# Scatter token numbers, expert 1's second matrix in four pieces, and routing sums ahead of the turns

## The chip, the cores and the metric

The kernel runs on one core of one Trainium2 chip. The core has five instruction streams that run side by side and wait for one another through semaphores: TensorE (PE in the profile, with its weight loads as PEld), VectorE (DVE), ScalarE (ACT), GpSimd (POOL) and SyncE (SP, which here only issues DMA transfers). Each stream works in its own order: an instruction that waits holds back everything behind it on that engine. TensorE writes into PSUM banks, of which the program has eight.

The metric is the device time of one execution, in microseconds, and the median over executions.

## The reference

A long convolution along the sequence is followed by a layer of eight experts of which every token uses one.

```python
X = np.fft.rfft(x, axis=1)                      # x: 8 x 3072 x 256
y = np.fft.irfft(X * (filt_r + 1j * filt_i)[None], n=3072, axis=1)
x = y.reshape(24576, 256)
logits = x @ w_gate                             # 8 experts
expert_idx = np.argmax(logits, axis=1)
gate_w = softmax(logits)[chosen expert]
...
for i in range(N):                              # first 768 tokens of each expert
    e = expert_idx[i]
    if counts[e] < capacity:                    # capacity 768
        disp[e, counts[e]] = x[i]; pos[i] = counts[e]; counts[e] += 1; keep[i] = True
h = np.maximum(np.einsum('ecd,edf->ecf', disp, w1), 0.0)   # w1: 8 x 256 x 1024
y = np.einsum('ecf,efd->ecd', h, w2)                       # w2: 8 x 1024 x 256
out[i] = gate_w[i] * y[expert_idx[i], pos[i]]   # 0 for tokens that were not kept
```

## The kernel before

Only the first tokens of each expert count, so the kernel convolves three batches of eight (the third for half of its rows), routes their tokens, and computes the experts; a branch at the end does the whole again if an expert was not full by then, which does not happen with these inputs.

**The order of the work is the order of the code.** The whole kernel stands in a manual schedule: each engine gets its instructions in the order in which the Python code emits them, and the framework adds the waits. The functions named below emit; `run` calls a list of emitters, `interleave` mixes lists.

**A batch's convolution.** `rows_in` (lines 889 to 895) emits the first transform (matmuls L273, copies to `ZA`). `cv.t(k)`, the turns, transpose `ZA` into `Q` (matmuls L296, copies L301 on ScalarE); there are six. `cv.middle` (from line 360) then goes through six groups g of frequencies, each in two halves h. `b(g, h)` emits the matmuls L309 on `Q`, four VectorE products L325 for the two halves of a group, and a subtraction and an addition on GpSimd (L329, L330) that give `t`. `g(u)` emits twelve matmuls L342 on `t` and copies `yh`, `yl`; it needs up to two groups' `t`, both halves. `bi(u)` emits nine matmuls L356 and copies into `V`. `middle` takes a list `fill` of other work and puts one item of it behind each half group. After the middle come the transposes `ti`, and the second inverse transform `ai` or, for the last batch, `ai_last` (matmuls L414, L440, copies to `rt`, DMA writes of `rt` to `ybuf`).

**Routing.** `route` returns lists: `counts` (VectorE: argmax, one-hot, running sums, ending in `ends`), `sums` (five small matmuls, L509 to L512, on `ends`), `slots` (VectorE, from L517 on), `masks` (one-hot tables for the index table, L560 to L562) and `table` (matmuls L570, then a finish into `tacc`, a table that has for every slot of every expert its row in `ybuf`). For batches 0 and 1, `cv.t(0)` is emitted between `counts` and `sums`.

**Token numbers.** Rows of `ybuf` are not in token order. `row_of_slot` makes gather indices from `tacc` with one VectorE instruction. `scatter_rows(ix, n)` (lines 696 to 725) makes the token numbers, to which results are scattered, with eighteen VectorE instructions in a chain. For the first twelve columns of the table (experts 0 and 1, `idxs0`) it is called in `early_index`, an item of `fill` in the last batch's middle; for all 48 (`idxs`) it is called after the convolution, ahead of expert 1's first up steps.

**Experts.** Slots come in chunks of 384. `gather` brings a chunk's rows with three indirect DMAs on GpSimd (L590). `turn` transposes them on TensorE (L604) and splits them into a high and a low part, `xh` by ScalarE (L611) and `xl` by VectorE (L615). An up step is six matmuls L630 (high by high, low by high, high by low), a ReLU split into `h` (L611 ScalarE, L613 VectorE); a chunk has eight. A down step is 24 matmuls L681 and a scaled copy `ob` (L684); `scatter` is an indirect DMA on GpSimd (L687). Expert 0's first chunk and expert 1's first chunk are computed early, from the first two batches' tokens, among the last batch's transforms.

**Weights.** `load_part` loads a matrix (1 MB) into a raw tile and splits it in parts by `cut`: `wah` (or `wbh`) by a ScalarE copy, the low part by a GpSimd subtraction (L744, for expert 1's first matrix), or by a ScalarE negation (L746) and a later accumulating DMA (L750). The pool `raw0` has one buffer, so expert 1's second matrix goes where its first matrix lay. Before, it comes as one DMA that GpSimd issues (L737) after the four subtractions. ScalarE's order there is: two copies `rt`, two cuts of the second matrix, two copies `rt`, a cut, an `ob`, a cut, and then `xh` of the turn of expert 1's first chunk.

Of the kernel before, what the change touches and what calls it, by code (L numbers as in the profile page):

```python
# [9 lines left out]
F32 = mybir.dt.float32  # L10
# [11 lines left out]
N1, N2, NP = 96, 32, 24  # L22
# [71 lines left out]
def fftconv_moe_kernel(ctx, tc, x, x0, fr, fi, fny, wg, w1, w2, ca, cai, cb, co, out, cap):  # L94
    nc = tc.nc
    NB, SEQ, D = x.shape[0], N1 * N2, 256
    E, FF = w1.shape[0], w1.shape[2]
    NT = (cap + 127) // 128
    NSLOT = E * NT
# [63 lines left out]
    def interleave(*lists):  # L163

        marks = sorted(((i + 1) / (len(l) + 1), j, i) for j, l in enumerate(lists) for i in range(len(l)))
        for _, j, i in marks:
            lists[j][i]()

    def run(fs):
        for f in fs:  # L170
            f()
# [521 lines left out]
    def down(k, ix=None):  # L693
        run(down_steps(k, ix))
# [31 lines left out]

    def load_part(e, part, raw, pool, parts=2, dma=None, add=True, adds=None):

# [6 lines left out]
        def load():  # L735
            box.append(raw.tile(shape, F32, name="raw", tag="raw"))
            (dma or nc.sync).dma_start(out=box[0], in_=src)  # L737

        def cut(k):
# [101 lines left out]
    with tc.manual_schedule():  # L841
# [55 lines left out]
        for b in range(NB0 - 1):  # L897
# [10 lines left out]
            interleave(rows_in(b + 1, range(4, 8), False), counts)  # L908
            cv.t(0)
            sums()  # L910
            interleave([lambda k=k: cv.t(k) for k in range(1, NP // 4)], slots)
            if b + 2 == NB0:
# [17 lines left out]
        def early_index():  # L930
            early_count()
            row_of_slot(idx0, EE * NT)
            scatter_rows(idxs0, EE * NT)

# [20 lines left out]
        adds, scatters = [], []  # L955
        load_a, cut_a = load_part(1, "a", raw0, w1p, 4, add=False)
        load_b, cut_b = load_part(1, "b", raw0, w1p, 4, nc.gpsimd, adds=adds)
        load_a()
        L = new_L(True)
# [13 lines left out]
        run([early[4], cut_a[0], early[5], cut_a[1], early[6], cut_a[2], early[7], cut_a[3]])  # L973
        load_b()
        for q in range(2, 4):
# [7 lines left out]
        sums()  # L983
        run(scatters[:1])
        run(cut_b[:2])
# [3 lines left out]
        later[1]()  # L989
        run(scatters[1:2])  # L990
        run(cut_b[3:])
        run(masks)
        X[1, 0] = turn(early_x[1], NE, ep1)
        later[2]()
# [15 lines left out]
        R[1, 1] = load_rows(1, 1)  # L1010
        scatter_rows(idxs, NSLOT)

# [13 lines left out]
        load_a()  # L1026
        down((1, 0), idxs0)
        up((1, 1), list(cut_a), 1)
        down((0, 1))
# [117 lines left out]
```

## Time and profile before

| | |
|---|---|
| median of 3 runs | 489.73 us |
| the runs | 489.97, 489.73, 486.75 us |
| the profiled execution, its own time | 493.15 us |
| its span in the trace | 491.3 us |
| mean granted clock of TensorE | 0.991 of full speed |
| TensorE busy | 473.9 us, 96% of the span |
| VectorE, ScalarE, GpSimd busy | 49%, 54%, 40% of the span |

TensorE is busy almost throughout; matmuls are pipelined, so busy says that matmuls are under way, not that they go at full speed. The granted clock says at which of its two levels, 1.2 or 2.4 GHz, TensorE ran: 1.00 is 2.4 GHz, 0.50 is 1.2 GHz. A row of the timeline has its start, its duration, engine, line, operation, tiles, shape, and in brackets how long the engine was idle before it and what ended that.

### The profile page before, as it was taken

How to read it: one execution, taken by the hardware profiler on the slowest of the kernel's cores; microseconds unless marked ns; L12 is line 12 of the kernel's file. 1: busy time of each engine (PE TensorE's matmuls, PEld its weight loads, DVE VectorE, ACT ScalarE, POOL GpSimd, SP SyncE). 2: the span in 40 equal slices, each digit the busy share in tenths (PEclk: the TensorE clock that was granted, in tenths of full speed). 3: DMA queues.
4: the chain of work that ended last, by engine and by line, in shares of the span. 5: the costliest groups of instructions: out<-in, count | busy, mean ns of one | idle time of the engine just before them, and what ended most of it. 6: DMA issues, size and time to landing. Idle time of an engine off the chain costs nothing.

```text
span 491.3 us, 10853 instructions
## 1 busy us (share of the span) xinstructions
PE 473.9 (96%) x4317; PEld 462.2 (94%) x4317; DVE 240.2 (49%) x562; ACT 264.7 (54%) x618; POOL 198.8 (40%) x241
## 2 busy tenths in 40 slices
PE   8999999999999899989999999999999999999994
PEld 8999998999989799979899999999999899999994
DVE  3587755776557788847422343233332323423510
ACT  3555767356576587554362684374383482573421
POOL 3064210552104674618432654355354454454022
PEclk9999999999999899999999999999999999999999
DMA  8996180990817738547348699979979989985001
GB/s 291 391 312 257 33 234 4 256 345 2 234 39 211 171 61 179 141 144 152 82 141 233 145 235 268 357 196 273 355 213 263 362 211 271 376 159 123 1 24 48
DMA packets 59980, 95.72 MB, mean 195 GB/s; under 512 B 4016, under 2 KB 36496, under 8 KB 59792
## 3 DMA queue, kind: packets, MB, share of 16 engines
q1 hardware_dynamic: 43264, 63.27, 39.6%
q0 software_dynamic: 15344, 29.56, 28.2%
q10 hardware_dynamic: 1312, 2.10, 1.3%
q8 instruction: 36, 0.59, 0.5%
q14 instruction: 24, 0.20, 0.1%
HBM read 54.81 MB, written 40.11 MB: 193 GB/s over the span
## 4 chain that ended last, share of the span: by engine, by line
PE 48%; issue 21%; POOL 11%; DMA 11%; ACT 4%; DVE 2%; POOLq 1%; SPq 0%; ACTq 0%
PE ps L630 9%; PE ps L273 9%; DMA y<-ob,idxs 7%; PE ps L681 7%; PE ps L342 6%; PE ps L309 6%; PE ps L414 5%; PE ps L356 5%; POOL y L687 4%; POOL rows L590 3%; DMA raw<-w 2%; POOL wal L750 2%; PE ps L296 1%; POOL wbl L750 1%; DMA V<-x 1%
## 5 line engine op out<-in xcount | busy, mean ns | idle before, releaser
L681 PE MATMUL ps<-wbh,h 128*128 128x256 f32 x768 | 139.5, 281 | 0.2
L613 DVE SCALAR_TENSOR_TENSOR h<-ps,h 128x384 fp32r<-128x384 f32 x128 | 66.8, 553 | 120.1 <-ACT h L611 99.6
L681 PEld LDWEIGHTS ps<-wbh,h 128*128 128x128 f32 x768 | 119.1, 189 | 1.1 <-issue 0.7
L681 PE MATMUL ps<-wbl,h 128*128 128x256 f32 x384 | 107.6, 280 | 0.4 <-issue 0.4
L687 POOL DMA_INDIRECT y<-ob,idxs x48 | 48.1, 1003 | 115.0 <-ACT ob L684 108.6
L630 PE MATMUL ps<-xh,wah 128*128 128x384 f32 x256 | 87.2, 341 | 3.7 <-ACT xh L611 2.0
L630 PE MATMUL ps<-xl,wah 128*128 128x384 f32 x256 | 87.0, 340 | 0.6 <-DVE xl L615 0.2
L630 PE MATMUL ps<-xh,wal 128*128 128x384 f32 x256 | 86.6, 338 | 0.0
L611 ACT ACTIVATE h<-ps 128x384 fp32r<-128x384 f32 x128 | 58.8, 497 | 46.2 <-PE ps L630 38.4
L681 PEld LDWEIGHTS ps<-wbl,h 128*128 128x128 f32 x384 | 72.7, 189 | 0.9 <-issue 0.9
L684 ACT ACTIVATE ob<-ps,gt 128x256 f32<-128x256 f32 x48 | 22.1, 477 | 77.3 <-DMA y<-ob,idxs 36.7
L630 PEld LDWEIGHTS ps<-xh,wah 128*128 128x128 f32 x256 | 48.6, 190 | 4.9 <-ACT ob L684 2.6
L329 POOL TENSOR_TENSOR t<-t,t 128x256 f32<-128x256 f32 x33 | 24.9, 753 | 67.8 <-DVE t L325 63.4
L630 PEld LDWEIGHTS ps<-xl,wah 128*128 128x128 f32 x256 | 48.6, 190 | 1.4 <-DVE xl L615 0.9
L630 PEld LDWEIGHTS ps<-xh,wal 128*128 128x128 f32 x256 | 48.7, 190 | 0.0
L590 POOL DMA_INDIRECT rows<-ybuf,idxg x42 | 42.4, 1009 | 15.1 <-issue 12.2
L342 PE MATMUL ps<-IG,t 128*128 128x136 f32 x288 | 39.0, 285 | 2.5 <-POOL t L330 2.4
L345 ACT CAST yh<-ps 128x408 fp32r<-128x408 f32 x48 | 23.9, 502 | 29.7 <-PE ps L342 28.4
L342 PEld LDWEIGHTS ps<-IG,t 128*128 128x128 f32 x288 | 36.3, 194 | 3.2 <-POOL t L330 3.1
L309 PE MATMUL ps<-Bc,Q 128*128 128x128 f32 x288 | 36.3, 278 | 0.0
L615 DVE TENSOR_TENSOR xl<-ps,xh 128x384 fp32r<-128x384 f32 x32 | 16.2, 547 | 38.8 <-ACT xh L611 30.5
L309 PEld LDWEIGHTS ps<-Bc,Q 128*128 128x128 f32 x288 | 33.8, 192 | 0.9 <-issue 0.7
(142 smaller groups left out, 746.0 us busy)
## 6 DMA issues: line engine op xcount, KB each, us to landing
y<-zt SPq DMA_DIRECT2D x12, 2048.0 KB, 20.1
raw<-w SPq DMA_DIRECT2D x13, 1024.0 KB, 7.1
wbl<-w POOLq DMA_DIRECT2D x16, 512.0 KB
wal<-w POOLq DMA_DIRECT2D x14, 512.0 KB
xt<-x SPq DMA_DIRECT2D x16, 384.0 KB, 4.5
ybuf<-rt SPq DMA_DIRECT2D x12, 256.0 KB, 4.6
ybuf<-rt SPq DMA_DIRECT2D x14, 204.0 KB, 3.5
Q<-x SPq DMA_DIRECT2D x4, 528.0 KB, 9.2
```

What stands on the lines that cost most here:

```text
L273: nc.tensor.matmul(ps[:, i * w:(i + 1) * w], xt[:, i, h * 128:(h + 1) * 128], A[:, i * QP:i * QP + w], start=True, stop=True)
L309: nc.tensor.matmul(ps[:, i * 128:(i + 1) * 128], self.Q[:, p, h * 128:(h + 1) * 128], self.Bc[:, 1 if p == NP - 1 else 0, :], start=True, ...
L329: eng.tensor_tensor(out=t1[:, :, 0, :], in0=t1[:, :, 0, :], in1=t2[:, :, 1, :], op=ALU.subtract)
L342: nc.tensor.matmul(ps[:, i * 136:(i + 1) * 136], self.ysb[(p // 4, h)][:, (p % 4) * 128:(p % 4 + 1) * 128], self.IG[:, h, :], start=True, ...
L356: nc.tensor.matmul(ps[:, :272], w[:, m, :], y[:, i, :], start=k == 0, stop=k == 2)
L414: nc.tensor.matmul(ps[s * rows:(s + 1) * rows, i * w:(i + 1) * w], AI[:, o, r0:r0 + rows], V[h][:, :w // 2, o, :], start=True, stop=True)
L590: nc.gpsimd.indirect_dma_start(out=rows[:, t, :], out_offset=None, in_=yrows[:lim, :], in_offset=bass.IndirectOffsetOnAxis(ap=idx[:, j + t ...
L611: nc.scalar.activation(out=hi, in_=ps, func=AF.Relu if relu else AF.Copy)
L613: nc.vector.scalar_tensor_tensor(out=lo, in0=ps, scalar=0.0, in1=hi.bitcast(F32), op0=ALU.max, op1=ALU.subtract)
L630: nc.tensor.matmul(ps[:, :n * 128], w[:, kk, m * 128:(m + 1) * 128], y[:, kk, o], start=k == 0, stop=k == 5)
L681: nc.tensor.matmul(ps[:, :D], y[:, m, o], w[:, m, :], start=m == 0 and j == 0, stop=m == NF - 1 and j == 2)
L687: ins = nc.gpsimd.indirect_dma_start(out=out, out_offset=bass.IndirectOffsetOnAxis(ap=(idxs if ix is None else ix)[:, j:j + 1], axis=0), i ...
```

## The change

Five edits, all in the order of emission but one. (1) `early_index` no longer calls `scatter_rows(idxs0, ...)`; it is called after `masks` of the last batch, and the first two scatters of expert 0 are emitted right behind it instead of where their `ob` is made. (2) `scatter_rows(idxs, NSLOT)` moves from ahead of expert 1's up steps to behind the down steps of its first chunk. (3) Expert 1's two matrices share one flat raw tile; the second comes in four pieces of 256 KB on SP's queue, each into the quarter that one cut of the first matrix has read, in place of one load on GpSimd's queue. (4) In batches 0 and 1 `sums()` is emitted ahead of all turns. (5) With that, the six turns, not five, are interleaved with `slots`.

```diff
-    def load_part(e, part, raw, pool, parts=2, dma=None, add=True, adds=None):
+    def load_part(e, part, raw, pool, parts=2, dma=None, add=True, adds=None, flat=None):
...
+        def load_piece(k, parts):
+            n = shape[1] // parts
+            nc.sync.dma_start(out=box[0][:, k * n:(k + 1) * n, :], in_=src[:, k * n:(k + 1) * n, :])
+
+        if flat is not None:
+            box.append(flat.rearrange("p (n f) -> p n f", f=shape[2]))
+            load = load_piece
...
-            cv.t(0)
             sums()
-            interleave([lambda k=k: cv.t(k) for k in range(1, NP // 4)], slots)
+            interleave([lambda k=k: cv.t(k) for k in range(NP // 4)], slots)
...
             row_of_slot(idx0, EE * NT)
-            scatter_rows(idxs0, EE * NT)
...
-        load_a, cut_a = load_part(1, "a", raw0, w1p, 4, add=False)
-        load_b, cut_b = load_part(1, "b", raw0, w1p, 4, nc.gpsimd, adds=adds)
-        load_a()
+        flat = raw0.tile([128, 8 * D], F32, name="raw", tag="raw")
+        load_a, cut_a = load_part(1, "a", raw0, w1p, 4, add=False, flat=flat)
+        load_b, cut_b = load_part(1, "b", raw0, w1p, 4, adds=adds, flat=flat)
+        load_a(0, 1)
...
-        load_b()
+        for k in range(4):
+            load_b(k, 4)
...
         sums()
-        run(scatters[:1])
         run(cut_b[:2])
...
         later[1]()
-        run(scatters[1:2])
         run(cut_b[3:])
         run(masks)
+        scatter_rows(idxs0, EE * NT)
+        run(scatters[:2])
         X[1, 0] = turn(early_x[1], NE, ep1)
...
         R[1, 1] = load_rows(1, 1)
-        scatter_rows(idxs, NSLOT)
...
         down((1, 0), idxs0)
+        scatter_rows(idxs, NSLOT)
```

The first place is VectorE in the last batch's middle, behind the table's finish. Before, the end of the eighteen instructions (te, tf and up are their work tiles) and then the products of group 2:

```order
L722 TENSOR_SCALAR up<-at 128x12
L706 SCALAR_TENSOR_TENSOR tf<-up,tf 128x12
L724 TENSOR_SCALAR te<-tacc 128x12
L725 TENSOR_TENSOR idxs_73<-te,tf 128x12
L325 TENSOR_TENSOR t_2356<-ps,FRT 128x512
```

and now:

```order
L451 TENSOR_SCALAR tb<-tb 128x1
L830 TENSOR_TENSOR tot<-tot,lack 128x2
L140 TENSOR_SCALAR idx_72<-tacc 128x12
L325 TENSOR_TENSOR t_2335<-ps,FRT 128x512
L325 TENSOR_TENSOR t_2336<-ps,FIT 128x512
```

The eighteen instructions are gone from there; the products stand right behind the gather index. They come back on VectorE between the one-hot tables of the last batch and the low part `xl` of expert 1's turn, whose end is now:

```order
L722 TENSOR_SCALAR up<-at 128x12
L706 SCALAR_TENSOR_TENSOR tf<-up,tf 128x12
L724 TENSOR_SCALAR te<-tacc 128x12
L725 TENSOR_TENSOR idxs_73<-te,tf 128x12
L615 TENSOR_TENSOR xl<-ps,xh 128x6x64 x2
L575 TENSOR_TENSOR tacc<-tacc,pr 128x48
```

where before L615 followed the one-hot tables directly. The second place is GpSimd behind the four subtractions for expert 1's first matrix. Before:

```order
L744 TENSOR_TENSOR wal<-raw,wah 128x512 x4
L737 DMA raw<-w 128x8x256
L445 COPY L<-rt_2860 128x48
L445 COPY L<-rt_2879 128x48
L445 COPY L<-rt_2898 128x32
L687 DMA y<-ob,idxs_73 24576x256 x2
L590 DMA rows<-ybuf,idxg 128x264 x3
```

On SP's queue, between the load of expert 1's first matrix and the last batch's writes, stands now:

```order
L741 DMA raw<-w 128x2x1024
L741 DMA raw<-w 128x2x256 x4
L446 DMA ybuf<-rt_2841 128x6x136
L446 DMA ybuf<-rt_2860 128x6x136
L446 DMA ybuf<-rt_2879 128x4x136
```

The load has left GpSimd's row and become four on SP's, ahead of five writes to `ybuf`; the two scatters keep their place in GpSimd's row, between the copies of the logits and the gathers, but wait there for `idxs0`.

## Rows read from the trace of the kernel before

**Rows 1.** The page, part 1: busy time of each engine.
```profile
PE 473.9 (96%) x4317; PEld 462.2 (94%) x4317; DVE 240.2 (49%) x562; ACT 264.7 (54%) x618; POOL 198.8 (40%) x241
```
**Rows 2.** Windows of 3 us: stretch, length, busy by engine, clock, DMA share, GB/s.
```profile
169.00:172.00 3.00, 3.00 (x16) 3.00 (x15) 0.64 (x2) 1.57 (x8) 2.68 (x4) 0.51 0.85 135
220.00:223.00 3.00, 3.00 (x11) 3.00 (x10) 2.20 (x13) 1.10 (x3) 2.06 (x2) 0.50 0.18 45
```
**Rows 3.** Timeline, TensorE, middles of batch 1 and of the last batch.
```profile
92.57 1.56 PE L342 MATMUL ps<-IG,t 128*128 128x136 f32 x12
...
105.54 1.95 PE L309 MATMUL ps<-Bc,Q 128*128 128x128 f32 x16
...
156.11 1.56 PE L342 MATMUL ps<-IG,t 128*128 128x136 f32 x12
...
167.99 0.50 PE L342 MATMUL ps<-IG,t 128*128 128x136 f32 x2 [2.22 <-POOL t L330]
...
173.58 1.95 PE L309 MATMUL ps<-Bc,Q 128*128 128x128 f32 x16
```
**Rows 4.** Timeline, VectorE, last batch's middle: first of eighteen, and what follows them.
```profile
159.54 0.17 DVE L708 TENSOR_SCALAR tf<-tacc 128x12 f32<-128x12 f32 x1
...
162.44 0.68 DVE L325 TENSOR_TENSOR t<-ps,FRT 128x512 f32<-128x512 f32 x1
```
**Rows 5.** Timeline, GpSimd, last batch's middle: group 2's first, group 3's last operation.
```profile
163.81 0.72 POOL L329 TENSOR_TENSOR t<-t,t 128x256 f32<-128x256 f32 x1 [3.13 <-DVE t L325]
...
173.54 0.74 POOL L330 TENSOR_TENSOR t<-t,t 128x256 f32<-128x256 f32 x1
```
**Rows 6.** Timeline, TensorE, start of expert 1's first chunk.
```profile
216.28 0.17 PE L827 MATMUL ps<-tot,ones 128*1 128x10 f16 x1
218.47 0.44 PE L630 MATMUL ps<-xh,wah 128*128 128x384 f32 x1 [2.02 <-ACT xh L611]
...
228.02 0.59 PE L604 MATMUL ps<-ident,rows 64*128 64x64 f32 x12
```
**Rows 7.** Chain that ended last: eight up steps, start and duration.
```profile
249.31 8.32 PE ps L630 x48
```
**Rows 8.** Timeline, ScalarE, ahead of expert 1's first chunk.
```profile
207.46 0.59 ACT L442 COPY rt<-ps 128x512 f32<-128x512 f32 x1 [0.47 <-PE pr L512]
212.06 0.62 ACT L742 CAST wbh<-raw 128x512 fp32r<-128x512 f32 x1 [4.01 <-DMA raw<-w]
...
217.55 0.87 ACT L611 ACTIVATE xh<-ps 128x384 fp32r<-128x384 f32 x2
```
**Rows 9.** Timeline, GpSimd: four subtractions, then the load.
```profile
196.46 5.08 POOL L744 TENSOR_TENSOR wal<-raw,wah 128x512 fp32r<-128x512 f32 x4 [1.54 <-ACT wah L742]
...
201.83 0.94 POOL L737 DMA_DIRECT2D raw<-w  x1 [0.30 <-POOL wal L744]
```
**Rows 10.** Timeline, VectorE, end of the one-hot tables and the low part.
```profile
212.10 0.35 DVE L562 TENSOR_TENSOR ohh<-ohh,nv 128x384 f16<-128x384 f16 x1
218.07 1.02 DVE L615 TENSOR_TENSOR xl<-ps,xh 128x384 fp32r<-128x384 f32 x2 [5.61 <-ACT xh L611]
```
**Rows 11.** Timeline, GpSimd: the last of twelve gathers in a row.
```profile
239.23 1.00 POOL L590 DMA_INDIRECT rows<-ybuf,idxg  x1 [0.31 <-issue]
```
**Rows 12.** DMA, 238 to 244 us in forty slices: busy tenths.
```profile
DMA  0096271000398450000991740000000000000000
```
**Rows 13.** Timeline, batch 0: first turn, the read of the sums, first table.
```profile
77.29 0.28 PE L296 MATMUL ps<-ident,ZA 64*128 64x64 f32 x2
...
78.83 0.17 DVE L517 COPY bs<-pr 128x16 f32<-128x16 f32 x1 [4.25 <-PE pr L512]
...
83.75 0.38 PEld L570 LDWEIGHTS <-ol 128*128 128x128 f16 x8 [0.20 <-DVE ohh L560]
```
**Rows 14.** Windows of 5 us, columns as in group 2.
```profile
245.00:250.00 5.00, 5.00 (x42) 5.00 (x41) 0.43 (x1) 1.06 (x3) 2.01 (x2) 1.00 0.74 262
...
385.00:390.00 5.00, 3.83 (x22) 3.51 (x21) 2.58 (x6) 3.60 (x9) 2.56 (x3) 1.00 1.06 400
```

## The prediction

> **What bounds the kernel now.** I read the page's busy times first: TensorE is busy for 96% of the span, no other engine for more than 54% [rows 1]. So a change can gain only where TensorE stands still or runs at its lower clock. The windows of 3 us over the stretch that the diff touches come next: in two places the granted clock is 0.51 and 0.50, that is 1.2 GHz, and VectorE, ScalarE and GpSimd aren't full in these windows [rows 2]. The timeline then says what came before each: a TensorE wait of 2.22 us in the last batch's middle, ended by GpSimd's t [rows 3], and one of 2.02 us ahead of expert 1's first chunk, ended by ScalarE's xh [rows 6]. Nothing else in the stretch comes near these.
>
> What the first place costs can be read without a model, because batch 1 does the same middle without the extra work. From the first L342 to the matmuls L309 of group 4 it takes 105.54 - 92.57 = 12.97 us in batch 1 and 173.58 - 156.11 = 17.47 us in the last batch [rows 3]. The loss is 4.50 us: 2.22 of waiting, the other 2.28 mostly matmuls at half the clock.
>
> For the second place, TensorE is done with the tables at 216.28 + 0.17 = 216.45 and turns the next rows (L604) at 228.02 [rows 6], 11.57 us later. Between lie seven up steps; eight take 8.32 us in an undisturbed stretch [rows 7], so seven take 7.28. The loss is 4.29 us: 2.02 of waiting, the rest the lower clock and a short second wait for xl.
>
> The profiled execution took 493.15 us in all, 3.42 above the median of 489.73. I take savings as differences from the profiled one and subtract them from the median.
>
> **The change, part by part.**
>
> *Token numbers for experts 0 and 1 leave the middle.* The eighteen instructions run on VectorE from 159.54, and the products of group 2 start at 162.44, so these come 2.90 us earlier [rows 4]. GpSimd waits 3.13 us for just these products and then works without a wait from 163.81 to 173.54 + 0.74 = 174.28: four pairs of additions, three gathers, one weight transfer, 10.47 us [rows 5]. It can start 2.90 us earlier, at 160.91, and end at 171.38. TensorE's wait of 2.22 us is for the second half of group 2, early in this row, which then is done before TensorE asks for it. What is late next: TensorE would reach group 4's L309 at 173.58 - 4.50 = 169.08, finish them 1.95 us later at 171.03 [rows 3], and then needs group 3's last addition, which GpSimd gives at 171.38. So I give back 0.4 us: the part is worth 4.50 - 0.4 = 4.1 us. If TensorE simply follows GpSimd, it is worth 2.9; with no wait left, 4.5. These are its ends.
>
> *The same instructions come back ahead of xl.* Behind the one-hot tables (end 212.10 + 0.35 = 212.45) VectorE now has 2.90 us of them, to 215.35, and then the two xl, 1.02 us [rows 10]. Before, VectorE idled 5.61 us there, so the cover exists; but the cover is now nearly used up. Behind them wait xl, hence TensorE, and two scatters on GpSimd.
>
> *Expert 1's second matrix in pieces.* The whole load is issued at 201.83, after the fourth subtraction, and ScalarE, which had idled 4.01 us, starts cutting it at 212.06 [rows 8, 9]: 10.23 us. ScalarE's xh stands behind the four cuts and starts at 217.55. Now piece k needs only subtraction k. The four subtractions take 5.08 us, 1.27 each, so they end at 197.73, 199.00, 200.27 and 201.54. A load of 256 KB doesn't occur in the trace. Its upper bound is the 10.23 us of the whole matrix, which gives 207.96, 209.23, 210.50 and 211.77; its lower bound is nothing beyond the issue. ScalarE is free for the first cut at 207.46 + 0.59 = 208.05. Even at the upper bound only the second cut waits, for about 0.1 us. So the size of a piece doesn't matter here, and I count no cost. From the first cut to the start of xh ScalarE now needs 217.55 - 212.06 = 5.49 us, without a wait; from 208.05 it reaches xh at 213.54 and ends it at 214.41.
>
> The larger of the two is VectorE: xl ends at max(215.35, 214.41) + 1.02 = 216.37. TensorE is free at 216.45. So neither xh nor xl is waited for, by 0.1 us. I take the whole 4.29 us, as 4.3; its lower end is 2.0, where only the wait goes and the clock still falls.
>
> *What comes behind.* The next thing that TensorE needs from outside is three gathered row tiles for its turn, which it now asks for at 216.45 + 7.28 = 223.73. Their index is ready some 0.7 us after xl, at about 217.1. GpSimd is held by the two scatters, which wait for the token numbers at 215.35. A gather takes 1.00 us and the next follows after 0.31 [rows 11], and I take the same for a scatter: scatters to 217.97, gathers to about 221.6. After the last gather, issued by 240.23, the DMA engines are busy until about 241.5 [rows 12], 1.3 us more: 222.9. That leaves 0.8 us.
>
> SP's queue gets four transfers ahead of five writes of ybuf. The last piece is issued at about 201.6, so writes that were ready earlier wait up to a microsecond. They gate only these gathers, which GpSimd keeps until 218 anyway.
>
> *Token numbers of all slots* move to where VectorE is busy for 0.43 of 5 us [rows 14]. Four microseconds fit; cost nothing. Where they stood, VectorE was not what TensorE waited for; gain nothing.
>
> *Sums ahead of the turns.* In batch 0 VectorE had idled 4.25 us when the sums came, that is since 74.6, and TensorE reaches the first turn at 77.29, so the sums can run 2.7 us after their input is there. VectorE's slots then start about 1.2 us earlier, and the first table's wait of 0.20 us can go [rows 13]. ScalarE's copies of the turns are not moved. Two batches give 0 to 0.4 us; I take 0.2, since a new bound by ScalarE's copies may take its place.
>
> **Sum.** 4.1 + 4.3 + 0.2 = 8.6 us: 493.15 - 8.6 = 484.6 for a profiled execution, 489.73 - 8.6 = 481.1 for the median. The lower ends give 2.9 + 2.0 + 0 = 4.9, so 484.8; the upper ones 4.5 + 4.3 + 0.4 = 9.2, so 480.5.
>
> **Rivals.**
>
> *Only the first place is cured.* VectorE's chain clears TensorE's need by 0.1 us and the gathers by 0.8. If either is late by 2 us, TensorE stands as before and the clock falls as before: the gain is 4.1 + 0.2, so 485.4. For it speaks the tight cover; against it that each estimate leans on durations in this trace, and that lateness under a microsecond costs only itself. 0.10.
>
> *The pieces come no earlier than the whole did*, because what mattered was the wait and not the queue or the quarter. Then xh is at 217.55 as before: again 485.4. The rows speak against it: the DMA was issued when its one buffer came free, 0.30 us after the last subtraction [rows 9], and three of the pieces are allowed earlier than that. The Trainium skill, "DMA: Bandwidth & Descriptors", section "Issuing engines are not separate DMA queues", says that starting DMAs from another engine saves only the time it takes to issue them. By that rule the change of queue alone would save at most the 0.94 us of the issue, so 489.73 - 4.3 - 0.9 = 484.5; the quarters, not the queue, carry the rest of the sum. 0.04.
>
> *The time is given back later.* In the experts' stretch the DMA engines are full (share 1.06 from 385 to 390), and TensorE loses 1.17 us there [rows 14]. If that stretch ran by DMA, an earlier start would turn into waiting. Against it: TensorE loses no more than this, and loads there are started by TensorE's progress, so they shift too. Half of the gain lost gives 485.4, all of it 489.7; I say 487.5. 0.05.
>
> *Slower: the sums hold TensorE.* Ahead of the turns they stand first in TensorE's row, and all turns wait behind them. If the counts come more than 2.7 us later than now, each further microsecond is one of waiting, and a wait of about 2 us brings the lower clock, some 2.3 us as in the first place. Beyond a delay of about 4.7 us that costs 4.3 per batch, 8.6 for two, as much as the rest gains; at 8 us it gives 489.73 - 8.6 + 2 x (5.3 + 2.3) = 496.3. Nothing ahead of the counts moves in these batches, so 0.03.
>
> **How the numbers follow.** The forecast, 481.1, has the remaining 0.78. A difference of 1%, 4.9 us, is about what a measurement of this kernel can tell from no change. Faster by over 1% means below 484.8: the forecast, whose upper end just reaches that, and a little of the first two rivals, 0.80. Slower is the last rival, 0.03. Between lie 0.17. The range starts at 479.5, a microsecond below the upper sum's 480.5 because the runs of before themselves spread over 3 us, and ends at 485.5 to hold the two rivals at 485.4.
>
> **What would show it.** In the changed kernel's profile the clock should be 1.00 in both places; the L342 matmuls behind group 3 should wait at most 0.5 us on GpSimd; the stretch from the first L342 to group 4's L309 in the last batch should be about 13 us; ScalarE's first cut of the second matrix should follow its copies without idling; xl should be ended by VectorE's own row, not by ScalarE; the eight up steps behind it should take about 8.3 us. I am wrong if xl or the gathers come late enough to drop the clock again, or if the experts' stretch grows.

## The result and the profile after

The changed kernel takes 483.88 us (median of 6, 482.97 to 485.86), the kernel before beside it 489.65 us (6 runs, 486.75 to 491.03): a ratio of 0.9894 with an interval of 0.9862 to 0.9927. The medians lie 5.8 us apart; the ratio, which is not the quotient of the medians, stands for 5.2 us (3.6 to 6.8). The profiled execution took 483.88 us, exactly the median, with a span of 482.0 us and a mean clock of 0.998. That of before took 493.15 with a span of 491.3 and a mean clock of 0.991. It is none of the six that the median of before is of; on three other chips, below, the median of the same kernel was 492.5 to 493.5 us, so its 3.4 us above 489.73 may belong to the occasion as well as to the execution. From trace to trace the change saves 9.3 us, from median to median 5.8. Where these two part is the main question of what follows.

The page of the changed kernel, busy time of each engine and the granted clock in forty slices of the span:

```profile
PE 470.8 (98%) x4317; PEld 460.4 (96%) x4317; DVE 240.4 (50%) x562; ACT 264.2 (55%) x618; POOL 198.1 (41%) x240
...
PEclk9999999999999999999999999999999999999999
```

TensorE has 3.1 us less of busy time than in [rows 1] for the same 4317 matmuls, and no slice shows a lowered clock. The two places of [rows 2] in windows:

```profile
169.00:172.00 3.00, 2.80 (x25) 2.60 (x24) 2.29 (x6) 1.94 (x7) 2.78 (x4) 1.00 0.96 187
...
218.00:221.00 3.00, 3.00 (x26) 2.61 (x25) 1.55 (x4) 1.73 (x4) 3.00 (x3) 1.00 0.38 95
```

**First place.** TensorE's and GpSimd's timelines in the last batch's middle, for [rows 3] and [rows 5]:

```profile
156.16 1.56 PE L342 MATMUL ps<-IG,t 128*128 128x136 f32 x12
...
164.07 1.58 PE L342 MATMUL ps<-IG,t 128*128 128x136 f32 x12
...
169.13 1.95 PE L309 MATMUL ps<-Bc,Q 128*128 128x128 f32 x16
...
171.52 1.43 PE L342 MATMUL ps<-IG,t 128*128 128x136 f32 x10 [0.20 <-POOL t L330]
```
```profile
160.91 0.74 POOL L329 TENSOR_TENSOR t<-t,t 128x256 f32<-128x256 f32 x1 [0.17 <-DVE t L325]
...
170.72 0.74 POOL L330 TENSOR_TENSOR t<-t,t 128x256 f32<-128x256 f32 x1
```

The matmuls at 164.07 are those that waited 2.22 us. From the first L342 to group 4's L309 it is now 169.13 - 156.16 = 12.97 us, exactly what batch 1 takes in [rows 3]. GpSimd starts at 160.91, as computed, and ends at 170.72 + 0.74 = 171.46, where 171.38 had been computed; TensorE then waits 0.20 us for it.

**Second place.** TensorE, ScalarE, VectorE, SP's queue and GpSimd ahead of expert 1's first chunk, each from its own timeline, for [rows 6] and [rows 8 to 10]:

```profile
212.38 0.17 PE L835 MATMUL ps<-tot,ones 128*1 128x10 f16 x1
212.47 0.44 PE L630 MATMUL ps<-xh,wah 128*128 128x384 f32 x1
...
219.96 0.74 PE L604 MATMUL ps<-ident,rows 64*128 64x64 f32 x12
```
```profile
203.89 1.07 ACT L442 COPY rt<-ps 128x512 f32<-128x512 f32 x2 [2.09 <-DMA ybuf<-rt]
204.85 0.63 ACT L750 CAST wbh<-raw 128x512 fp32r<-128x512 f32 x1
...
210.33 0.89 ACT L611 ACTIVATE xh<-ps 128x384 fp32r<-128x384 f32 x2
```
```profile
208.25 0.17 DVE L708 TENSOR_SCALAR tf<-tacc 128x12 f32<-128x12 f32 x1
...
211.14 1.01 DVE L615 TENSOR_TENSOR xl<-ps,xh 128x384 fp32r<-128x384 f32 x2
```
```profile
193.78 4.16 SPq L741 DMA_DIRECT2D raw<-w  x4
198.04 7.31 SPq L446 DMA_DIRECT2D ybuf<-rt  x4
```
```profile
212.06 1.03 POOL L687 DMA_INDIRECT y<-ob,idxs  x1 [12.94 <-DVE xl L615]
...
217.36 1.01 POOL L590 DMA_INDIRECT rows<-ybuf,idxg  x1 [0.30 <-issue]
```

TensorE goes from the tables straight into the up steps; from 212.55 to L604 it takes 7.41 us instead of 11.57. VectorE ends xl at 211.14 + 1.01 = 212.15, 0.4 us before TensorE is free; ScalarE's xh ends 0.9 us earlier still. The first scatter starts at 212.06, 0.9 us behind the token numbers, which are done when xl starts; the prediction had it follow at once, and the 0.8 us that it gave the gathers covered that. The last gather is issued by 218.37 and the turn at 219.96 doesn't wait. ScalarE shows a wait that wasn't there before: 2.09 us for a write of `ybuf` to give back its tile `rt`. These writes stand behind the four pieces on SP's queue. It delays the first cut and nothing that TensorE waits for.

**The sums.** In batch 0 they now run ahead of the turns (timeline, TensorE):

```profile
77.25 0.17 PE L509 MATMUL pr<-ends,tri 128*128 128x8 f16 x1
...
81.27 0.71 PE L296 MATMUL ps<-ident,ZA 64*128 64x64 f32 x15 [0.22 <-ACT Q L301]
83.81 0.52 PE L570 MATMUL pr<-ohh,ol 128*128 128x96 f16 x8
```

The first table starts at 83.81, in [rows 13] at 83.75: its wait for VectorE is gone, and the turns wait on ScalarE's copies of `Q` as long.

### The profile page after: what moved, and what is told of

The parts are those of the page before. It is cut to its first block, busy times and chain, and to the rows that moved or that the text cites. A ratio compares the mean times of both kernels' runs of the same rounds, so it can differ in the third digit from the quotient of the medians.

```text
span 482.0 us, 10856 instructions
## 1 busy us (share of the span) xinstructions
PE 470.8 (98%) x4317; PEld 460.4 (96%) x4317; DVE 240.4 (50%) x562; ACT 264.2 (55%) x618; POOL 198.1 (41%) x240
## 4 chain that ended last, share of the span: by engine, by line
PE 66%; issue 11%; DMA 8%; POOL 7%; ACT 4%; DVE 1%; POOLq 1%; SPq 0%; ACTq 0%
PE ps L630 18%; PE ps L681 14%; PE ps L273 9%; DMA y<-ob,idxs 7%; PE ps L342 6%; PE ps L309 5%; PE ps L414 5%; PE ps L356 4%; POOL y L687 2%; PE ps L440 2%; POOL wal L758 1%; PE ps L296 1%; DMA V<-x 1%; POOL rows L590 1%; ACT Q L301 1%
## 5 line engine op out<-in xcount | busy, mean ns | idle before, releaser
L342 PE MATMUL ps<-IG,t 128*128 128x136 f32 x288 | 38.0, 280 | 0.4 <-POOL t L330 0.4
L615 DVE TENSOR_TENSOR xl<-ps,xh 128x384 fp32r<-128x384 f32 x32 | 16.2, 547 | 42.9 <-ACT xh L611 42.8
L309 PE MATMUL ps<-Bc,Q 128*128 128x128 f32 x288 | 36.2, 278 | 0.0
L342 PEld LDWEIGHTS ps<-IG,t 128*128 128x128 f32 x288 | 35.3, 190 | 0.9 <-POOL t L330 0.8
L309 PEld LDWEIGHTS ps<-Bc,Q 128*128 128x128 f32 x288 | 33.8, 192 | 0.8 <-issue 0.7
```

Of the source, the lines that this page charges most:

```text
L309: nc.tensor.matmul(ps[:, i * 128:(i + 1) * 128], self.Q[:, p, h * 128:(h + 1) * 128], self.Bc[:, 1 if p == NP - 1 else 0, :], start=True, ...
L342: nc.tensor.matmul(ps[:, i * 136:(i + 1) * 136], self.ysb[(p // 4, h)][:, (p % 4) * 128:(p % 4 + 1) * 128], self.IG[:, h, :], start=True, ...
```

## The experiments

**The theories.** A: each place cost what the first profile of before showed, 4.5 and 4.3 us, and both are cured; what differs from execution to execution lies elsewhere. B: the places cost less in a usual execution than in the profiled one. C, the prediction's third rival: the gain is real, but part of it is given back in the experts' stretch. The twelve runs were made in three groups of four, each on one chip beside runs of the kernel before on it. The first group is the second profile of before, the first try to put the token numbers back, one load on GpSimd's queue and the two small moves put back (median of before 493.46 us); the second is the changed kernel again, the token numbers put back, one load on SP's queue and quarters on GpSimd's queue (492.98); the third is the last four runs (492.53). "Clock" without a place is the mean over an execution's span, averaged over all executions.

**A second profile of before.** The code is that of the kernel before.

> This is the kernel before, unchanged, to have a second profile of it. Theory (the two places cost what the first profile showed, and its 3.4 us over the median lie elsewhere): 489.6 us; in the profile 17.5 us from the last batch's first L342 to group 4's L309 and 11.6 us from the tables to L604, as before; if this profiled execution is shorter than 493, the difference lies behind L604, in the experts' stretch. Rival (the first profiled execution was an unlucky one at just these two places): the two stretches are together 2 to 3 us shorter than in the first profile.

Measured: 494.88 us, 1.0014 of the kernel before (0.9986 to 1.0041). The profiled execution took 494.82. TensorE's and ScalarE's timelines:

```profile
167.46 0.82 PE L342 MATMUL ps<-IG,t 128*128 128x136 f32 x2 [2.22 <-POOL t L330]
...
216.97 0.44 PE L630 MATMUL ps<-xh,wah 128*128 128x384 f32 x1 [1.31 <-ACT xh L611]
...
226.53 0.59 PE L604 MATMUL ps<-ident,rows 64*128 64x64 f32 x12
```
```profile
386.19 0.91 ACT L684 ACTIVATE ob<-ps,gt 128x256 f32<-128x256 f32 x2 [11.85 <-DMA y<-ob,idxs]
```

The first place is the same, 17.24 us with the same 2.22 us wait. The second is 0.7 us shorter, 10.86 us with a wait of 1.31: the load landed 9.51 us after its issue instead of 10.23. Behind L604 this execution is 266.5 us long, the first one 263.3. There ScalarE waits 11.85 us for a scatter to free one of four `ob`, and TensorE with it, in three waits of 4.5 us in all; in the first profile these were two waits of 1.5 us in all. So neither side holds as written: the first place is constant in the traces, the second moves by 0.7, and what sets these two traces apart most are the waits on `ob`.

All 29 executions of before on this chip have a mean clock, from 0.986 to 0.997, and their times follow it: a line through them falls by 4.8 us for each 0.01 of clock (0.01 of a span of 491 is 4.9). The averages of the two sets are 0.9919 and 0.9915. The two profiled executions had 0.991, the third (below) 0.990. So the second profile is a usual execution of its set in time and in clock, and it has the lowered clock in both places.

The mean clock is not the two places' alone. In each of the fourteen profiles the last 1.0 to 4.5 us of the span, in which TensorE has no work left, have a clock of 0.50; in the profile of the two small moves put back (window) that alone makes a mean of 0.995:

```profile
481.50:485.90 4.40, 0.00 (x0) 0.00 (x0) 0.00 (x0) 0.00 (x0) 0.00 (x0) 0.50 0.02 6
```

So the mean of a single execution doesn't say whether the clock was lowered in one of the places. Averages are compared below; they are still rough.

**The changed kernel again.** The code is that of the changed kernel.

> The changed kernel, unchanged, on the chip of the runs beside it. Theory A (the two places gave what the first profiles showed, 4.1 and 4.2 us, and the rest of the difference between median and profile is scatter of the experts' stretch, which both kernels share): 8.2 us below the kernel before on the same chip, 0.983 of it. Theory B (the second place is worth less in a usual execution, since the load of the second matrix often lands earlier than in the first profile: 3.0 or less): 5.8 to 7 below, as measured at first, 0.988. In both its profile has clock 1.00 in both places.

Measured: 488.26 us against 492.98, 4.7 us less by the medians; ratio 0.9888 (0.9851 to 0.9925), which stands for 5.5 us; in the profiled execution the places take 12.97 and 7.41 us, as at first. B's ratio, not A's. The clock rises from 0.9930 (24 executions of before, 0.988 to 0.999) to 0.9967: 0.0037 of 490 us is 1.8 us (0.9 to 2.7 by the scatter of the executions). The two traces of before and after would give 0.007, 3.4 us.

**The token numbers put back.** The edit, in `early_index` and behind `masks`:

```diff
             row_of_slot(idx0, EE * NT)
+            scatter_rows(idxs0, EE * NT)
...
-        scatter_rows(idxs0, EE * NT)
         run(scatters[:2])
```

> The changed kernel with the token numbers of experts 0 and 1 back in the last batch's middle; the rest stays changed. Theory (each part is worth what the place lost in the first profile): 483.9 + 4.1 = 488.0 us, with a TensorE wait of about 2.2 us on GpSimd's t in the last batch's middle and a clock near 0.5 behind it, 17.5 us from the first L342 to group 4's L309. Rival (in a usual execution the places cost only about two thirds of that, 5.8 us for both): 483.9 + 2.8 = 486.7.

In the run tokens_back the added call stood outside `early_index`: the numbers come ahead of the whole last middle, from a table that isn't finished, so that results go to wrong rows. As a kernel with the token numbers in neither place it took 486.92 us, 0.9866 (0.9837 to 0.9895), with 12.95 and 7.44 us in the two places, as the changed kernel. With the call inside:

> The changed kernel with the token numbers of experts 0 and 1 back in the last batch's middle (in the run tokens_back they had come ahead of that middle by mistake, from an unfinished table); the pieces and the rest stay changed. Theory: the changed kernel + 4.1 us, 17.5 us from the last batch's first L342 to group 4's L309, a wait of some 2 us on GpSimd's t and a clock near 0.5 behind it. Rival (part of that comes back in the second place, where VectorE is then free ahead of xl): + 2.9 or less.

Measured: 491.66 us, 0.9958 (0.9929 to 0.9986), 3.4 us above the changed kernel beside it. TensorE, timeline and window:

```profile
170.59 0.50 PE L342 MATMUL ps<-IG,t 128*128 128x136 f32 x2 [2.23 <-POOL t L330]
```
```profile
171.00:174.00 3.00, 3.00 (x17) 3.00 (x16) 1.24 (x3) 1.77 (x7) 2.68 (x4) 0.59 0.74 134
```

In the trace it is 17.52 us instead of 12.97, the 4.5 of theory A; in the medians 3.4. The second place doesn't give anything back (7.44 us), so the rival's reason is not the cause. The clock is 0.9939 on average, from 0.991 to 0.998: 0.0028 below the changed kernel, 1.4 us, and with 2.2 us of waiting 3.6. This kernel also says what the rest of the change is worth, the second place above all: its first place is as before, its second is cured, and its ratio of 0.9958 stands for 2.1 us (0.7 to 3.5), where the prediction has 4.3 + 0.2. Its clock is only 0.0009 above that of the kernel before, 0.4 us, where the lowered clock of the second place costs 1.8 in a trace (below).

**The second matrix: queue and quarters.** Three kernels, each the changed one with another load. One load on GpSimd's queue, as before (one load on SP's queue has the first of the diff's three places alone; quarters on GpSimd's queue have the other two alone):

```diff
-        for k in range(4):
-            load_b(k, 4)
+        load_b(0, 1)
...
-            nc.sync.dma_start(out=box[0][:, k * n:(k + 1) * n, :], in_=src[:, k * n:(k + 1) * n, :])
+            (dma or nc.sync).dma_start(out=box[0][:, k * n:(k + 1) * n, :], in_=src[:, k * n:(k + 1) * n, :])
...
-        load_b, cut_b = load_part(1, "b", raw0, w1p, 4, adds=adds, flat=flat)
+        load_b, cut_b = load_part(1, "b", raw0, w1p, 4, nc.gpsimd, adds=adds, flat=flat)
```

> The changed kernel with expert 1's second matrix loaded whole from GpSimd's queue, as before; the rest stays changed. Theory: 483.9 + 4.3 = 488.2 us; the first cut waits for the load some 4 us, TensorE waits about 2 us for xh and runs at half the clock behind it, some 11.6 us from the tables to L604. Rival (two thirds of it): 483.9 + 2.9 = 486.8. Second rival (with the first place cured the load is issued early enough, so that this edit was worth nothing): 483.9.

> The changed kernel with expert 1's second matrix as one load on SP's queue: the queue is changed, the quarters are not. Theory (the wait for all four subtractions and the size decide, not the queue): the first cut waits for the load some 3 us as with the one load on GpSimd's queue, which landed 9.0 us after its issue; TensorE waits 0.7 to 1.3 us for xh, the changed kernel + 0.7 to 1.3 us. Rival (the queue decides: on SP's queue the load needs no 0.94 us of GpSimd and lands early): no wait for xh, within 0.3 of the changed kernel.

> The changed kernel with the four quarters issued from GpSimd's queue, behind its four subtractions: the quarters are changed, the queue is not. Theory (a quarter lands sooner than the whole, some 5 us after its issue): the first cut waits at most 1 us, TensorE does not wait for xh; but four issues of 0.94 us instead of one hold back GpSimd's copies of L by 2.8 us, of which VectorE's earlier wait ahead of the sums covers about 1.2, so the tables come up to 1.6 us later: the changed kernel + 0 to 1.6 us. Rival (a quarter takes as long as the whole, 9 us): the cuts are as late as with one load or later, TensorE waits 1 to 4 us for xh and the clock falls: + 1.3 to 5 us.

Measured: one load on GpSimd's queue 488.33 us, 0.9881 (0.9846 to 0.9915); one load on SP's queue 488.76, 0.9901 (0.9865 to 0.9937); quarters on GpSimd's queue 488.45, 0.9905 (0.9874 to 0.9935). The changed kernel, beside the last two, 488.26, 0.9888. No difference among these four can be told from the medians. The timelines can: GpSimd, ScalarE and TensorE with one load on GpSimd's queue,

```profile
198.64 0.94 POOL L741 DMA_DIRECT2D raw<-w  x1 [0.30 <-POOL wal L752]
...
207.67 0.62 ACT L750 CAST wbh<-raw 128x512 fp32r<-128x512 f32 x1 [3.03 <-DMA raw<-w]
...
214.08 0.45 PE L630 MATMUL ps<-xh,wah 128*128 128x384 f32 x1 [0.73 <-ACT xh L611]
```

SP's queue, ScalarE and TensorE with one load on SP's queue,

```profile
198.21 0.37 SPq L741 DMA_DIRECT2D raw<-w  x1
...
206.28 1.07 ACT L442 COPY rt<-ps 128x512 f32<-128x512 f32 x2 [3.82 <-DMA ybuf<-rt]
207.24 0.63 ACT L750 CAST wbh<-raw 128x512 fp32r<-128x512 f32 x1
...
213.67 0.44 PE L630 MATMUL ps<-xh,wah 128*128 128x384 f32 x1 [0.56 <-ACT xh L611]
```

and GpSimd and ScalarE with quarters on GpSimd's queue:

```profile
197.14 2.96 POOL L741 DMA_DIRECT2D raw<-w  x4
...
203.38 0.62 ACT L750 CAST wbh<-raw 128x512 fp32r<-128x512 f32 x1
```

With one load on either queue the first cut starts 9.0 us after the issue and xh comes too late, by 0.73 and 0.56 us; the second place takes 8.74 and 8.55 us. But the waits differ. On GpSimd's queue the cut waits for the load: its packets end at 207.12, 8.5 us after the issue. On SP's queue they end at 204.16, 5.95 us after it, and no cut waits for them; by 203.3, before the first write of `ybuf` moves, 903 of its 1024 packets are through (DMA view, 198.2 to 203.3: packets, MB, share):

```profile
q1 hardware_dynamic: 903, 0.92, 64.7%
```

There ScalarE is held for 3.82 us by a tile `rt`, whose write to `ybuf` stands behind the load on the same queue; the cuts stand behind that copy. So the theory of the second run has the time about right and the wait wrong, and its rival has the load right and the outcome wrong. With quarters on GpSimd's queue the first quarter is there at most 6.2 us after the start of the issues, which come as late as the whole load's, no write stands behind them, and TensorE doesn't wait; the place takes 7.41 us, as with SP's queue. With quarters on SP's queue the issues start at 193.78 instead of 198.21, ahead of the last subtraction, so the writes behind them hold `rt` for 2.09 us instead of 3.82. So quarters cure the rest of the place on either queue, and a change of queue alone trades one wait for another.

The Trainium skill, "DMA: Bandwidth & Descriptors", section "Issuing engines are not separate DMA queues", has it that another issuing engine saves only the issue's time. TensorE's wait keeps to that, 0.2 us less where the issue took 0.94. The landing in these traces doesn't, it is 2.5 us sooner: the first packet comes 1.03 instead of 2.63 us after the issue, and the packets take 4.9 instead of 5.9 us, ahead of the writes instead of beside them.

A cost that was expected of the third run didn't come: GpSimd's four issues take 2.96 us and its copies of L end 3.4 us behind the subtractions instead of 1.8, but nothing that TensorE needs waits for them.

What was not expected: with one load the place is 1.1 to 1.3 us longer, not 4, and the clock stays at 1.00. In the traces of before the load landed after 10.23 and 9.51 us and TensorE waited 2.02 and 1.31; with the token numbers out of the middle it landed, on the same queue, after at most 9.0. Why it lands earlier there wasn't tried; what shows is that in this place waits of 0.56 and 0.73 us had no lowered clock behind them and waits of 1.31 to 2.02 us had one.

**The two small moves put back.**

```diff
+            cv.t(0)
             sums()
-            interleave([lambda k=k: cv.t(k) for k in range(NP // 4)], slots)
+            interleave([lambda k=k: cv.t(k) for k in range(1, NP // 4)], slots)
...
         R[1, 1] = load_rows(1, 1)
+        scatter_rows(idxs, NSLOT)
...
         down((1, 0), idxs0)
-        scatter_rows(idxs, NSLOT)
```

> The changed kernel with the sums behind the first turn again and the token numbers of all slots ahead of the up steps again; the two large edits stay. Theory (the copies of ScalarE bound the tables, and VectorE has room in either place for the slots' token numbers): 483.9 us, within 0.3. The prediction's term: 483.9 + 0.2 = 484.1. Rival (these two carry the 1.2 us that the changed kernel gained behind L604): 485.1.

Measured: 487.53 us, 0.9865 (0.9835 to 0.9895), beside 0.9888 and 0.9894 of the changed kernel: no loss, where the rival asked for a ratio of some 0.0025 more. In batch 0 the first table starts at 83.89 instead of 83.81.

**What a late xl costs, and what the clock alone costs.** Late: the changed kernel computes the token numbers twice ahead of xl. Filled: the kernel before gets useless matmuls in its two waits (`fillers` is an empty dictionary, filled for the last middle alone).

```diff
         scatter_rows(idxs0, EE * NT)
+        scatter_rows(idxs0, EE * NT)
         run(scatters[:2])
```
```diff
                     p, h = u * 3 + (3 * k + i) // 2, (3 * k + i) % 2
+                    for _ in range(fillers.get((u, k, i), 0)):
+                        nc.tensor.matmul(ps[:, 408:], zt[:, :128], zt[:, :104], start=True, stop=True)
...
+        fillers[2, 1, 2] = 10
         cv.middle(V, fill, ahead, last=[early_turn])
...
         full_flag()
+        ps = bank()
+        for _ in range(5):
+            nc.tensor.matmul(ps[:, :128], zt[:, :128], zt[:, :128], start=True, stop=True)
```

> The changed kernel with the eighteen instructions of the token numbers done twice ahead of xl, the second time for nothing: xl and both scatters come 2.9 us later. Theory (the cover was as thin as forecast: xl ended 0.4 us before TensorE was free of the tables): TensorE waits about 2.3 us for xl, the clock falls behind it, some 2 us more, and the gathers come up to half a microsecond late: the changed kernel + 4.3, about 0.9975 of the kernel before. Rival (the clock stays): + 2.3 to 2.8, about 0.994.

Measured: 490.62 us, 0.9975 (0.9950 to 1.0001), the theory's number. TensorE, timeline and window:

```profile
214.83 0.52 PE L630 MATMUL ps<-xl,wah 128*128 128x384 f32 x1 [2.30 <-DVE xl L615]
```
```profile
216.00:219.00 3.00, 3.00 (x12) 3.00 (x12) 1.09 (x5) 1.12 (x3) 2.37 (x3) 0.59 0.24 87
```

The place takes 11.55 us, 4.14 more than in the changed kernel: 2.30 of waiting and 1.84 of the clock. The averages say the same: the clock is 0.9933, 0.0034 below the changed kernel's 0.9967, 1.7 us. The cover of 0.4 us that the change leaves is real: of the 2.9 us that VectorE is given 2.5 lie beyond it, and they cost 4.1.

> The kernel before with useless matmuls of zeros in TensorE's two waits: ten ahead of the one matmul that waits for the second half of group 2 in the last batch's middle (about 2.0 us of the 2.22), five between the tables and expert 1's first up step (about 1.25 of the 1.3 to 2.0). The data still come when they came. Theory (half of each place's loss is the lower clock, and it is TensorE's standing still that brings it): no fall of the clock in either place; 15.2 us instead of 17.4 from the first L342 to group 4's L309, 1.6 to 2.0 us less from the tables to L604; 2 to 4 us below the kernel before, 0.992 to 0.996 of it. Rival (the clock falls for another reason, or idle time alone is the price): the clock falls as before, 1.000 of it.

Measured: 491.99 us, 1.0001 (0.9972 to 1.0030): not the theory's 2 to 4 us. Yet the trace shows what the theory said (timeline, and windows of the two places):

```profile
165.74 2.37 PE L345 MATMUL ps<-zt 128*128 128x104 f32 x20
168.14 0.50 PE L346 MATMUL ps<-IG,t 128*128 128x136 f32 x2
```
```profile
168.00:171.00 3.00, 2.97 (x26) 2.86 (x24) 1.67 (x3) 2.08 (x8) 2.69 (x4) 1.00 0.88 187
217.00:220.00 3.00, 3.00 (x19) 3.00 (x18) 2.24 (x14) 1.22 (x4) 1.75 (x2) 1.00 0.11 21
```

The data come when they came, TensorE is kept busy, and the clock stays at 1.00. The first place takes 15.90 us instead of 17.47, so 1.6 us of its loss were the clock and the other 2.9 the wait that is only filled; the second takes 8.53 instead of 10.86 to 11.57. So the standing still does bring the lower clock. On average the clock rises from 0.9931 to 0.9956, clear of the scatter (0.0013 to 0.0037), but that is 1.2 us, and the interval of 1.4 us to either side can't tell 1.2 from nothing. The forecast of 2 to 4 us was read from profiled executions, where the averages give 1.2; whether even that arrives in the time is not shown.

**Eight buffers for `ob`.** Both kernels, in the experts' stretch behind the early chunks alone:

```diff
-            ob = sm["p"].tile([128, D], F32, name="ob", tag="ob", bufs=4)
+            ob = sm["p"].tile([128, D], F32, name="ob", tag="ob", bufs=8 if "nrows" in sm else 4)
```

> The changed kernel with eight buffers instead of four for the output tiles ob of the experts' stretch, where ScalarE waits up to 12 us for a scatter to free one, and TensorE with it for 0 to 2.6 us at one chunk and 0 to 1.5 at another, in some executions more than in others. Theory (these waits are what spreads the executions and part of the time): no TensorE wait on ob behind L604 over 0.3 us, 1 to 3 us below the changed kernel, 0.983 to 0.987 of the kernel before, with less spread. Rival (the DMA engines are full there, and TensorE waits as long for the next weights): within 0.3 us of the changed kernel, 0.989.

> The kernel before with the same eight buffers; at once a third profile of the two places. Theory: 1 to 3 us below the kernel before, 0.994 to 0.998, as much as the same edit gives behind the change, so that the change gives nothing back in the experts' stretch; the two places cost what they did, 17.4 us and 10.9 to 11.6. Rival (part of the change's gain is given back at ob): the edit gives 2 us more to the changed kernel than to this one.

Measured: with the change 484.14 us, 0.9841 (0.9808 to 0.9873); without it 489.61, 0.9941 (0.9918 to 0.9965). TensorE's waits in the view of waits (total, times, longest), first the second profile of before, then the changed kernel with eight buffers:

```profile
PE ps L630 <- ACT ob L684: 4.5, 3, 2.6
PE ps L342 <- POOL t L330: 2.4, 2, 2.2
PE ps L630 <- ACT xh L611: 1.3, 1, 1.3
```
```profile
PE ps L681 <- issue: 1.0, 2, 0.7
...
PE ps L630 <- DVE xl L615: 0.6, 1, 0.6
...
PE ps L342 <- POOL t L330: 0.4, 2, 0.2
```

No wait on `ob` is left in either kernel with eight buffers, and the stretch behind L604 takes 261.8 (changed) and 261.2 us, the two shortest of all, though the first profile of the changed kernel with four buffers, 262.0, is near. The two places of the kernel before take 17.47 and 11.21 us, as its theory said. The edit gives the kernel before 2.9 us, and the changed one 0.9888 - 0.9841 to 0.9894 - 0.9841 of 492.53, that is 2.3 to 2.6, of which an interval of some 2 us either way leaves little sure. Theory C asked for 2 us more in the changed kernel. With eight buffers in both the change is worth 489.61 - 484.14 = 5.5 us, about 1 us either way by the scatter of the executions, as much as with four; and the changed kernel's profiles have waits on `ob` of 1.2 and 1.1 us in all, no longer than those of before, 1.5 and 4.5. So C falls. The changed kernel with eight buffers is the fastest of all, 8.4 us below the kernel before.

## Why the prediction was right, and where its sum was too large

The direction, the two places and their mechanism were right: faster, by 5.8 and 4.7 us from median to median and by 5.2 and 5.5 us by the ratios, where 8.6 was forecast, more than either interval allows; 483.88 lies within the range. Point by point:

- *Token numbers leave the middle, 4.1 us.* In the trace right to a tenth: 12.97 us instead of 17.47, less two waits of 0.20 us. By the medians 3.4, by the ratios 3.5, some 2 us either way.
- *Second place, 4.3 us.* Cured in full in the trace, 7.41 us instead of 11.57. In the time it is worth half of the forecast: with the first place left as it was, all that remains of the change gives 2.1 us (0.7 to 3.5). The trace of before that sized it had the longest wait of three: 2.02, 1.31 and, in the kernel with eight buffers, 1.65. And the pieces alone are worth 1.1 to 1.3 us in the traces, too little to be told in the medians; with the token numbers moved, most of the place is already cured.
- *VectorE's cover.* 0.1 us forecast, 0.4 measured; the price when it is gone 4.1 in the trace, about what the first rival had (4.3). That lateness under a microsecond costs only itself was near: with one load on GpSimd's queue waits of 0.73 and 0.23 us made the place 1.33 us longer.
- *Pieces.* No cut waits for its quarter. The writes of `ybuf` behind them on SP's queue, said to gate the gathers alone, also hold ScalarE's tile `rt`: 2.09 us, which xh could spare, and 3.82 behind one whole load, which it could not.
- *Sums ahead of the turns, 0.2 us.* Nothing: ScalarE's copies are the bound, the reason that was named for taking only half.
- *Token numbers of all slots, nothing.* Nothing.

**The step that was mis-sized** is "I take savings as differences from the profiled one and subtract them from the median", and with it both large terms, the second place's 4.3 most of all. By the prediction about half of each was the lower clock; the filled and the late runs put it at 1.6 of 4.5 and 1.8 of 4.1 us. The prediction took that part as every execution's. The averages of the granted clock say otherwise: between before and after they differ by 0.0037, 1.8 us, and not by the two places' 3.4; the first place has 1.4 of it (token numbers put back), the second 0.4. Reckoned anew, after the fact, with averages: waits that go, 2.22 + 1.3 to 2.0 + 0.24 for the second wait for xl, less 0.40 that come, are 3.4 to 4.1 us; clock 1.8 us; together an estimate of 5.2 to 5.9, about what was measured. Of the 9.3 us between the first two spans, 4.5 - 0.4 and 4.2 lie in the two places, and the rest is the waits on `ob` and other stretches behind L604, which differ from execution to execution of one kernel by more than that.

This account of the size is worked out from averages and not seen: all three profiles of before (one with eight buffers) have the lowered clock in both places, and no trace shows an execution of before without it. It also leaves out what the occasion may have added to the first profile, which belongs to no set of runs with a median of its own.

Theory A falls and C falls. B holds for the time and the clock of the second place; its reason, a load that lands earlier, holds only in part (9.51 and 9.85 us instead of 10.23, with the lowered clock all the same). Left open: why the clock would fall behind the same wait in some executions and not in others, and why the whole load lands earlier once the token numbers are moved.

## What to carry to other kernels

Before a loss read from one profile is subtracted from a median, see that the profiled execution is one of those that the median is of, and take several profiles: a loss made of a wait and a lowered clock is here sized best as the wait plus the difference in average clock times the span, with the idle end of the span in mind. An engine that is handed work ahead of an operand of the bound engine is safe up to its spare time and cost 4.1 us for 2.5 beyond it here, so work out the spare time first. A load moved to another queue also moves what stands behind it there: look at who waits for those transfers. When a transfer in pieces beats one transfer, test the pieces and the queue apart, and read which wait each leaves. Here the spread between executions led to something larger than either, four output buffers that waited for their scatters.

## What the runs showed of the hardware that was not expected

The length of a TensorE wait alone didn't decide whether the clock fell behind it. It fell to 0.5 or 0.6 behind waits of 2.22 to 2.23 us in the middle (in all four profiles that have one), of 2.30, 2.02, 1.65 and 1.31 ahead of expert 1's chunk, of 1.93 on `ob` (quarters on GpSimd's queue) and of 2.36 near the start (token numbers put back); it stayed at 1.00 behind waits of 2.56 and 1.48 us on `ob` in the second profile of before, of 1.86 on `ob` (one load on SP's queue) and of 2.06 near the start (one load on GpSimd's queue). What tells them apart these runs don't show.

In the second profile of before GpSimd issued four scatters, the first at 370.59 for 1.09 us, and the fifth `ob`, which takes the first one's tile, was written at 386.19: a scatter of 128 rows of 1 KB held its tile for 14.5 us after its issue while the DMA engines were full (share 1.12 from 371.68 to 386.19).
